# Another order of issue for the first phase of a layernorm, S4D convolution and gMLP kernel

## The chip, the cores and the metric

The kernel runs on one core of a Trainium2 chip. The metric is the device time of one execution in microseconds (us). A core has five engines that issue their own instruction streams in order: TensorE (PE, matmuls, with PEld for its weight loads), VectorE (DVE), ScalarE (ACT), GpSimd (POOL) and SyncE (SP, which here only issues DMA transfers). They wait for one another by semaphores.

## The reference

The input `u` has 2048 positions of 512 channels. A state space model (S4D) gives each channel a kernel K of 2048 taps, and the layernormed input is convolved with it; a gMLP block follows. Cut to what is computed:

```
A = -exp(log_A_real) + 1j * A_imag;  dt = exp(log_dt);  C = (C_real + 1j * C_imag) * dt
K = 2 * real(sum over n of C[d, n] * exp(A[d, n] * dt[d] * l))        # (512, 2048)
h = u + irfft(rfft(ln(u)) * rfft(K)) + ln(u) * D_skip
z = gelu(ln(h) @ w_in);  z1, z2 = halves of z
h2 = h + (z1 * (w_sp @ ln(z2) + b_sp)) @ w_out
```

## The kernel before

The first phase (`phase_a`, to 301.87 us) computes K and the convolution; the later phases, the gMLP, are the same in both kernels. The 512 channels are worked through in four chunks of 128, and a chunk in eight sequences of 16 channels. Fourier transforms are two stages of matmuls with constant matrices. The steps, with the names by which they appear in a row as written tile `<-` read tiles:

- `params` (DVE, ACT, a little POOL) makes the rates and coefficients of the channels' 128 modes, for chunk 0, then chunk 1, then chunks 2 and 3 together; results go through memory and come back by `stack` as `sw`. `table` (POOL, ACT) makes the factors `mt`.
- `norm_x` (DVE statistics, ACT or POOL for most normalising) layernorms u.
- `unit`, 32 of them, eight to a chunk, makes the taps of 16 channels. PE: the phase `ps<-c_k,sw`, two matmuls. ACT rounds, DVE takes the fraction `wb<-wb,ps`, ACT takes sines. POOL multiplies `m` from `mt`. DVE: three multiplies to `f`. PE: the first product `ps<-f`. DVE: the cosine multiply `wa<-ps,wa`, 128x1024. POOL: one more multiply. PE: the second product `ps<-wa,wb`. DVE or ACT: the copy to `ks`. Unit 13 is the sixth unit of chunk 1.
- `piece_a` (first transform stage of the input, PE `ps<-wb,big` for chunks 0 and 1 and `ps<-wb,wa` for 2 and 3, which `xt_load` brings back from memory as `wa<-scr_xhat`) and `piece_b` (second stage, PE `ps<-big,a` or `ps<-trio,a`, `128x64x2`), eight each per chunk, each followed by an evacuation from PSUM.
- `exchange`: eight DMA transfers per chunk on SP, `trio<-trio`, that swap the halves of the partitions. They go out as two groups of four, the second behind the last of the first. The exchange of a chunk needs its `piece_b` and every `piece_e` of the chunk before.
- `piece_c` (first stage of the taps, PE `ps<-wb,ks`, with an evacuation) and `piece_d` (second stage, PE `ps<-big,a`, `128x2x2x32`; then on DVE the spectral multiply `trio<-ps,trio`), which needs all eight `piece_c` and the exchange.
- `piece_e`: the inverse, PE `ps<-c_inv,trio`, 64 matmuls, with an evacuation to `big`. It needs all of the chunk's `piece_d`.

The order of all this is not the order of the code. `Plan` records each operation, 1380 in all, and `schedule` sorts them by a rank from the table `RANKS` (two digits in base 64 for each). `issue` then issues them one by one, so each engine gets its own in that order; every instruction of the phase has the line of `issue`, L249. Operations that two engines can do (evacuations, `ks` copies and the like on ACT or DVE; normalising on ACT or POOL; a few steps of `params` on DVE or POOL) are recorded with `either`, and the table `FORMS` has a digit for each choice. `BANKS` has a digit for each PSUM allocation: 0 and 1 are banks of 2x512 values, 2 to 5 of 512. The schedule touches nothing else; the waits follow from what the operations read and write in that order.

Of the kernel before, what the change touches and what calls it, by code (L numbers as in the profile page):

```python
# [33 lines left out]

DIGITS = "0123456789ABCDEFGHIJKLMNOPQRSTUVWXYZabcdefghijklmnopqrstuvwxyz+-"
RANKS = (
    "0600040901050F080B0A0b0Q0l0I0M070g0W03020C0E0G0H0J0K0L0N0O0R0V0Y0Z0c0U0d0e0n0i0m0q0t0w0z0+1112131416181J1T1w231+2628292D"
    "2E2H2K0y2J0-1K2N2P2b2X2e2V2j2u2z2p1Y1k1o2h2l2-0T0D0P0X0a0S0h0o0k0f331V371C10151W3c3N0s1O1c1r5X0j1p1l0p1j1n1q1g1D1B1U1P1m"
    "1X1b1A0x1H0u1I1h1i0r0v1Z1G1F1a171E1Q1R1u1y222527212A2F2L2O2Q2S2U2W2Y2a2c2d2g2i3I2s3L3Y2m3K3W3M3G2w2+382v423F3Q3l2n4N3V3r"
    "3q4P312r35323R3Z3A3D3T3y3p3O461v1f3B1-1S363E191e3C1x2t241s1z393H1N1d341M1L2q2x302M2G2o2R2I2y2k3J3P3g3k3m3X3s3t3x3z3-4043"  # L40
    "4547494B4D4E4H4G4R4I4T544S4x4h4W4f4M4j4u4m514s4U4V5P4k4o4K4Q5H4r4e4+4X574p4L4c4J4O594Y5a5Z5T6E692C2f2Z3S3e3+414Z4d4g4i4l"
    "4n4t4w5A5C5I5L5U5i5n5l5s5u6P6T4A655O5R6a6l746-777A6t6r6w6+5F5M5d6I797G3b3v4C444F4b6d8u8+909194989A9L9O9d9V9f9o9kAfAhAjAv"
    "AyB1BIAQB59GA5BOBxChCTCOCDC5CbC4CUCMC2CfCWCKCGC8CB9n9i9rAoEBEGBGEIEO555W585J4a4v5N5c5E5K4q4-52564z536U6c727C7n7s6G6N6368"
    "6x767q7-7D7J848h3U3d3i505D5S5Y3f2T205G5B5Q5m5b5g5r608X8i8r3a3h3o5j5q5+5x3j1t2B625y5w6M6J5-6Q6V6k8E8N3n3u4y646B6S6L5o5v6C"
    "6A6F6O6o6X6R6s707L979M3w61666i6v7873676Y6f717B6q7K7H7E7P7T7e9N9S7Q486K8m8w9T6D6W6g6n7F7W7Y6p756y6z7N7R7y7d7g818Q8a8d8o7I"
    "7O7V7b7h7x7v7M7Z7U7o7l7r88827z8B8G8k8x9C7f7k7u838H8L8q7t868A898C8K8-8R8z95999I9U9a7w878F8P8Z8g8l8S8M8I8c8Y8j8p8v8t92969B"
    "9E9J7+7m8b939pA15z6b5h5p5V5f5t6H5e5k6Z6h6j6u6e6m7i7p7S7a8O8V8T8f7c7j7X808J8U858D9m9s9+A79qA2A6AA9g9vACAHA9AD9t9yAbAkAUAc"
    "ALAnAwBNB2BFBTBcBhBsBMBkBpCZ9Z9e9lA4ABAGAK9c9Q9DAVARATAiAaAPAmArAxDBDKAFAJAMASAWAeAZ9Y9K9uAlAXAgBBAqAdBEBLBPCxD1ApAuA-B4"
    "B6BSBCAYAsAzB7B9BDBaBUBJBdBiBrCnD4AtA+B3BVBXBjBgBABZBRBYBeBbCCBnC0CFCNCeE3ECDG9xB0BfB+EMB8BKBQBlBqCPBwBWBmBtB-BvBzC-CdCH"
    "D3D8DCDPDeBHCICRCcCjCvCsC9CQCXCmC+CuD5DACwDHDQDTDaDkCtCzD2D9DJDXDOCoDED6DYDNDFDjDdDbDlDsE5E8EHD7DDDSDZDgDqDmD0DVDMDrDoDi"  # L50
    "DzDtDxE0E4E7EJESDICgDhEAETEk8W8n8e8s9F8y9H9z9P9R9W9X9b9j9hA3AEA89wA09-AIAOANBuCJBoC7CSCYCVCkCLCyC1CAByC3C6CEEcEjEVEbEYEd"
    "EiEpEuEzEoEvEfEnElEtFlFtFdFrF3FDFSFbGTGbFKFYG1GNGHGPGcH9DfDyE2E9EDENEKERDpD-EZEQELEwEUEmEyF9FUGpGwDwE1E6ErExF7F1EXEFEaF8"
    "F2F6FEFBF5FJFLFcGuGzEEEhFIFOFVFmFaEqF0FAFTFXFQFyFuFfF+G2G9GCGUFCFGFNFRFeFqFoFFFPFMFgFhFkFwFzFvG8GDGRGxH3FHEeFWFjGaGyFZFi"
    "FnFxG0G6GBFpG4GAG5GEGIGgGWGLGjGmGtHFHLFsG3G7GFGJGYGQF-GGGSGKGMGkH5GsGXH8HWHbHhHpGOGVGfGoH4HBHGH1GnGvH7H2G+HMHHHPHVHcHjHn"
    "HvGlG-HAHIHNHYHSGdHEHKHOHRHTHdHgHeHmHoHrHtHzGrGhH6I7IDIMCiCrCqCaCpClDLDUDRDWD+DcDnDuDvEPEgEWE+F4EsE-HJHaGZGiIRIcH0HDGeGq"
    "IOIUHQHXHwI3I0I5IFIQILISIIINIBIHI4IAI8IEIGIJIvJ2JuKCJ6JTJYJiJfJoIkJ7IYIgJNJxK2KfHZHfHkHqIKIWIPHUHsHlI2H-HyIfIbIVIiImIxKH"
    "KNHCHiHuH+I6I9IdI1ICHxIjIXInJ0ItIhJ3J9JCKVKgITIZIeIlIpI+IuIaIsIzIqIyJ4JHJDJ1JLJOJRK0K7IrIwI-J5JBJGJQIoJ8JEJAJIJMJmJUJbJp"
    "K4K5KLKxJFJJJPJVJdJnJhJKJSJXJlJaJcK6JtJkKAKYKnKqKwJWJZJeJjJqK1JvJgJ+JwJzK9J-KPKIK8KSKXKcKeKrJrJyK3KBKFKUKRJsKEKJKGKMKQKa"
    "KZKWKiKuKyK+L2KDKKKTKbKhKlKoKOKdKjKkKmKpKvKtKsKzK-L0L1L3L4L6L7LALBLHLGLJLCLFL5L8LELIL9LDLPLSLLLOLXLZLRLULKLMLNLQLTLWLVLY"
)  # L60
# [1214 lines left out]
```

## Time and profile before

| | us |
|---|---|
| median of three runs (839.03 to 842.73) | 839.1 |
| the profiled execution | 842.89 |
| span of its profile | 841.1 |
| first phase, to the first matmul of the next | 301.87 |
| PE, DVE, ACT, POOL busy in the span | 785.9, 650.9, 474.0, 300.7 |
| the same to 302 us | 254.28, 268.52, 246.80, 217.23 |

A row of the table of stretches gives a stretch from A to B in us, its length, the busy time of each engine with its number of instructions, the granted clock of TensorE as a share of full speed, the share of DMA time and GB/s. A row of a group gives the line, engine, operation, written and read tiles with their shape, and the count; behind the first bar the busy time of all in us and the mean of one in ns; behind the second the idle time ahead of them and who ended it. A row of the timeline or of the chain begins with the start and the length in us.

### The profile page before, as it was taken

What the parts mean: (1) busy time and instruction counts of PE and PEld (TensorE: products, weight loads), DVE (VectorE), ACT (ScalarE), POOL (GpSimd) and SP (SyncE); (2) the same over time, 40 slices, a digit from 0 to 9 for tenths busy, and PEclk for the clock granted to TensorE, in tenths of its full rate; (3) what the DMA queues carried; (4) which work ended last, traced back from release to release, by engine and by line L of the source; (5) the groups of instructions that cost most, each with busy time, mean ns of one, the idle gap of its engine ahead of it and who ended that gap; (6) DMA issues with size and microseconds to landing.
All of it is one profiled execution on the core that took longest, in us unless ns stands there. A gap on an engine that the chain in (4) does not pass through costs nothing.

```text
span 841.1 us, 20499 instructions
## 1 busy us (share of the span) xinstructions
PE 785.9 (93%) x8321; PEld 672.9 (80%) x8321; DVE 650.9 (77%) x1234; ACT 474.0 (56%) x795; POOL 300.7 (36%) x352
## 2 busy tenths in 40 slices
PE   0479999899999898999999999999999999999998
PEld 0278889688888898888999988888888878888887
DVE  6999999799998678663377689978856984888533
ACT  5799999789998235355223355555444443454111
POOL 5888959689877000000142100333231002232200
PEclk9999999999999999999999999999999999999999
DMA  9321613402205825445064045899799548799732
GB/s 333 95 104 41 137 40 68 113 19 53 63 3 116 327 54 138 138 138 190 36 151 125 1 150 141 186 222 222 188 209 217 152 140 202 149 249 236 166 111 77
DMA packets 64942, 115.71 MB, mean 138 GB/s; under 512 B 7024, under 2 KB 21488, under 8 KB 63952
## 3 DMA queue, kind: packets, MB, share of 16 engines
q1 hardware_dynamic: 53216, 93.04, 37.0%
q0 software_dynamic: 11632, 21.37, 15.6%
q8 instruction: 65, 1.06, 0.5%
q14 instruction: 29, 0.24, 0.1%
HBM read 86.59 MB, written 19.40 MB: 126 GB/s over the span
## 4 chain that ended last, share of the span: by engine, by line
PE 76%; DVE 11%; DMA 6%; issue 3%; ACT 2%; POOL 1%; SPq 1%; DVEq 0%; ACTq 0%; POOLq 0%
PE m L1163 26%; PE ps L249 24%; PE pz L958 9%; PE pz L852 9%; PE po L1086 5%; DVE trio L249 3%; PE pl L1086 2%; DMA zo<-scr_h 2%; DMA raws<-in_w_sp_dram 2%; DMA wa<-scr_xhat 1%; DMA trio<-in_par_dram 1%; DMA big<-in_u_a_dram 1%; DVE stats L753 1%; DVE big L249 1%; DVE wts L671 1%
## 5 line engine op out<-in xcount | busy, mean ns | idle before, releaser
L1163 PE MATMUL m<-wts,zc_wa 128*128 128x512 f32 x700 | 221.1, 395 | 0.0
L1163 PEld LDWEIGHTS m<-wts,zc_wa 128*128 128x128 f32 x700 | 131.7, 188 | 31.1 <-DVE c L1178 0.2
L1163 PE MATMUL m<-wts,zc_wb 128*128 128x512 f32 x350 | 138.1, 394 | 0.0
L1034 POOL DMA_DIRECT2D raws<-in_w_sp_dram x64 | 58.1, 971 | 212.0 <-DMA raws<-in_w_sp_dram 210.7
L249 POOL TENSOR_TENSOR wa<-mt 128x512 f32<-128x512 f32 x96 | 107.4, 1133 | 18.6 <-PE ps L249 15.4
L670 ACT CAST wts<-raws 128x512 fp32r<-128x512 f32 x112 | 69.0, 619 | 58.9 <-PE m L1163 30.7
L671 DVE TENSOR_TENSOR wts<-raws,wts 128x512 fp32r<-128x512 f32 x112 | 76.4, 684 | 20.0 <-ACT wts L670 19.9
L1163 PEld LDWEIGHTS m<-wts,zc_wb 128*128 128x128 f32 x350 | 65.8, 188 | 15.5
L958 PE MATMUL pz<-w,ht 128*128 128x448 f32 x384 | 77.0, 362 | 0.0
L958 PEld LDWEIGHTS pz<-w,ht 128*128 128x128 f32 x384 | 72.0, 187 | 4.9
L852 PE MATMUL pz<-ht,w1h 128*128 128x512 f32 (+1 forms) x248 | 74.2, 380 | 0.0
L964 POOL TENSOR_SCALAR sm<-sm 128x1 f32<-128x1 f32 x16 | 5.2, 326 | 183.5 <-DVE sm L963 183.5
L249 PEld LDWEIGHTS ps<-c_inv,trio 128*64 128x64 f32 x2048 | 63.0, 141 | 7.8 <-DVE trio L249 4.3
L249 PE MATMUL ps<-c_inv,trio 128*64 128x64 f32 x2048 | 65.4, 226 | 3.5 <-DVE trio L249 3.4
L1086 PE MATMUL po<-w,gz 128*128 128x512 f32 x252 | 61.8, 393 | 1.3 <-DVE zo L1126 1.3
L670 ACT CAST zc_wa<-raws 128x384 fp32r<-128x384 f32 (+1 forms) x70 | 36.9, 532 | 42.5 <-DVE raws L1068 25.6
L249 ACT ACTIVATE wb<-wb 128x1024 f32<-128x1024 f32 (+1 forms) x64 | 56.9, 891 | 0.9
L1086 PEld LDWEIGHTS po<-w,gz 128*128 128x128 f32 x252 | 47.3, 188 | 12.3 <-DVE zo L1126 1.7
L249 ACT ACTIVATE ps<-wb 128x1024 f32<-128x1024 f32 (+1 forms) x64 | 54.6, 859 | 3.1 <-DVE wb L249 1.3
L249 PE MATMUL ps<-big,a 128*128 128x128 f32 x448 | 54.5, 279 | 1.0 <-DVE big L249 0.9
L249 PEld LDWEIGHTS ps<-big,a 128*128 128x128 f32 x448 | 51.4, 192 | 3.5 <-issue 2.0
L852 PEld LDWEIGHTS pz<-ht,w1h 128*128 128x128 f32 x248 | 46.2, 193 | 8.8 <-ACT w1r L801 0.2
(168 smaller groups left out, 1530.0 us busy)
## 6 DMA issues: line engine op xcount, KB each, us to landing
raws<-in_w_sp_dram SPq DMA_DIRECT2D x112, 256.0 KB, 4.0
raws<-in_w_sp_dram POOLq DMA_DIRECT2D x80, 256.0 KB, 6.3
trio<-trio SPq DMA_DIRECT2D x32, 256.0 KB, 4.3
scr_z<-zo SPq DMA_DIRECT2D x28, 256.0 KB, 2.0
big<-in_u_a_dram SPq DMA_DIRECT2D x8, 512.0 KB, 7.3
xq<-in_u_b_dram SPq DMA_DIRECT2D x4, 1024.0 KB, 8.1
scr_h<-xq SPq DMA_DIRECT2D x16, 256.0 KB, 4.6
zo<-scr_z SPq DMA_DIRECT2D x14, 256.0 KB, 4.3
```

Source lines behind the costliest of these rows:

```text
L249: r = getattr(getattr(self.nc, e), method)(*map(self.real, args), **{k: self.real(x) for k, x in kw.items()})
L670: nc.scalar.copy(hi, src)
L671: nc.vector.tensor_sub(lo, src, hi.bitcast(F32))
L753: nc.vector.bn_stats(stats[:, n % 2, i, :], xqs[n % 3][:, i, :])
L852: nc.tensor.matmul(pt[:, w], a[:, q, f], ht[n][k][:, q, w], start=((q, i) == terms[0]), stop=((q, i) == terms[-1]))
L958: nc.tensor.matmul(pt[:, :FQ], a[:, q], w2[:, b, q, f], start=(q == 0 and i == 0), stop=(q == 3 and i == 2))
L964: nc.gpsimd.tensor_scalar_add(sm[:, 14:15], sm[:, 13:14], 1e-5)
L1034: nc.gpsimd.dma_start(r, ws[1], accum_op=ALU.add)
L1086: nc.tensor.matmul(pt, gz[fb][x][:, P * a:P * a + P], wo[:, y, fb, w], start=(first and fb == fbs[0] and i == 0), stop=(last and fb == fbs ...
L1163: nc.tensor.matmul(pt, x[:, f], y, start=(k == 0 and i == 0), stop=(k == KT - 1 and i == 2))
```

## The change

The three tables are replaced; there is no other edit. The operations and what they compute are the same. Each table is one long string, of which one line stands for the rest:

```diff
 RANKS = (
-    "0600040901050F080B0A0b0Q0l0I0M070g0W03020C0E0G0H0J0K0L0N0O0R0V0Y0Z0c0U0d0e0n0i0m0q0t0w0z0+1112131416181J1T1w231+2628292D"
...
+    "08020F0r1I0g0B0G0c0z1B0w1A0h1r3C4V1201000304070D0K0M0O0R0V0W0X0Y0a0d0Z0f0k090s0+0-1C1J1M0A0E0L0N0P0S0T0t0U0u100y1118161L"
...
 FORMS = (
-    "111111110001000111100111101100010000100011101000010011100011010111100000100111111111011010111110000110111101011000011001"
...
+    "111111110100001000101101011001001111110011000101000100100111001011110011011111111111110000011011101110011100010110101011"
...
 BANKS = (
-    "345452345244335544523535253025554240055110423005311052211552013400044010433330224523313242203203321123325421144400252114"
...
+    "335324233355242342422055322542444550040311455014550025210224115240034411252545452334235354545353342223543450123301425013"
```

Counted over the phase, DVE has 454 instructions before and 448 after: 67 evacuations and 54, 12 `ks` copies and 21, two steps of `params` fewer. ACT has 13 evacuations more and nine copies fewer. Around the middle, with the cosine multiply of unit 13 as the dividing point, the orders hold these numbers:

| | before | after |
|---|---|---|
| DVE up to and with that multiply | 303 | 286 |
| of them evacuations, `ks` copies, `params` | 35, 8, 56 | 21, 6, 55 |
| PE from the unit's second product to chunk 2's last `piece_e` | 105 | 130 |
| products, phases | 29, 15 | 33, 16 |
| `piece_a`, `piece_b` | 6, 8 | 11, 16 |
| `piece_c`, `piece_d`, `piece_e` | 13, 16, 16 | 14, 16, 23 |
| small ones | 2 | 1 |

**PE behind chunk 0's `piece_d`.** Before, from its last two `piece_d` on:

```order
L249 MATMUL ps2_100<-big_97,a2_78 128x2x2x32 x4
L249 MATMUL ps3_101<-big_97,a2_78 128x2x2x32 x4
L249 MATMUL ps0_98<-c_k_88,sw0_90 128x512 x2
L249 MATMUL ps2_100<-wb_87,wa_86 64x128 x8
L249 MATMUL ps3_101<-c_inv_60,trio_79 64x64 x32
L249 MATMUL ps2_100<-c_inv_60,trio_79 64x64 x32
L249 MATMUL ps1_99<-c_inv_60,trio_79 64x64 x32
L249 MATMUL ps4_102<-f2_96 32x64 x16
```

After, from some rows behind its last `piece_d` on:

```order
L249 MATMUL ps1_99<-c_k_88,sw1_91 128x512 x2
L249 MATMUL ps4_102<-f0_94 32x64 x16
L249 MATMUL ps3_101<-wb_87,wa_86 64x128 x8
L249 MATMUL ps4_102<-wa_86,wb_87 32x64 x16
L249 MATMUL ps2_100<-f1_95 32x64 x16
L249 MATMUL ps0_98<-c_k_88,sw1_91 128x512 x2
L249 MATMUL ps4_102<-c_inv_60,trio_79 64x64 x32
L249 MATMUL ps2_100<-wa_86,wb_87 32x64 x16
L249 MATMUL ps5_103<-c_inv_60,trio_79 64x64 x32
L249 MATMUL ps4_102<-wb_87,wa_86 64x128 x8
```

Before, the first inverses (`c_inv`) follow two rows behind the last `piece_d`. After, 16 rows stand between, units of chunk 1 and the first stage of chunk 2, and the last `wa,wb` row here is the second product of unit 13: one inverse is ahead of it, where before all eight were.

**DVE ahead of that multiply.** Before, the rows up to the cosine multiply of unit 13 (the last row):

```order
L249 COPY trio_79<-ps5_103 128x64x8
L249 TENSOR_TENSOR f1_95<-ps1_99,wa_86 128x512
L249 COPY big_97<-ps2_100 128x32x16
L249 TENSOR_TENSOR f1_95<-ps1_99,wa_86 128x512
L249 COPY trio_79<-ps3_101 128x64x8
L249 SCALAR_TENSOR_TENSOR f1_95<-wa_86,ps1_99 128x512
L249 SCALAR_TENSOR_TENSOR wb_87<-wb_87,ps0_98 128x1024
L249 COPY ks0_80<-ps3_101 128x256
L249 TENSOR_TENSOR wa_86<-ps5_103,wa_86 128x1024
```

After:

```order
L249 TENSOR_TENSOR wa_86<-ps3_101,wa_86 128x1024
L249 TENSOR_TENSOR f1_95<-ps0_98,wa_86 128x512 x2
L249 SCALAR_TENSOR_TENSOR f1_95<-wa_86,ps0_98 128x512
L249 COPY big_97<-ps5_103 128x128x4
L249 COPY ks0_80<-ps4_102 128x256
L249 SCALAR_TENSOR_TENSOR wb_87<-wb_87,ps1_99 128x1024
L249 TENSOR_TENSOR wa_86<-ps5_103,wa_86 128x1024
```

The evacuations of chunk 2's `piece_b` (`trio_79<-ps`) that stood among the unit's multiplies are no longer here.

**PE at chunk 2's inverses.** Before, the last four of the eight:

```order
L249 MATMUL ps5_103<-c_inv_60,trio_79 64x64 x32
L249 MATMUL ps1_99<-c_k_88,sw1_91 128x512 x2
L249 MATMUL ps4_102<-c_inv_60,trio_79 64x64 x32
L249 MATMUL ps3_101<-c_inv_60,trio_79 64x64 x32
L249 MATMUL ps2_100<-f0_94 32x64 x16
L249 MATMUL ps2_100<-wa_86,wb_87 32x64 x16
L249 MATMUL ps0_98<-c_k_88,sw1_91 128x512 x2
L249 MATMUL ps3_101<-c_inv_60,trio_79 64x64 x32
```

After:

```order
L249 MATMUL ps0_98<-c_k_88,sw1_91 128x512 x2
L249 MATMUL ps1_99<-c_k_88,sw1_91 128x512 x2
L249 MATMUL ps5_103<-c_inv_60,trio_79 64x64 x32
L249 MATMUL ps2_100<-c_inv_60,trio_79 64x64 x32
L249 MATMUL ps3_101<-c_inv_60,trio_79 64x64 x32
L249 MATMUL ps4_102<-c_inv_60,trio_79 64x64 x32
L249 MATMUL ps0_98<-f0_94 32x64 x16
L249 MATMUL ps3_101<-f1_95 32x64 x16
```

All phases of chunk 3 now stand ahead of the last four inverses, and the exchange of chunk 3 follows on them as before.

More of the change, by code (lines that the diff above doesn't have):

```diff
@@ L36 @@
 RANKS = (
-    "0600040901050F080B0A0b0Q0l0I0M070g0W03020C0E0G0H0J0K0L0N0O0R0V0Y0Z0c0U0d0e0n0i0m0q0t0w0z0+1112131416181J1T1w231+2628292D"
-    "2E2H2K0y2J0-1K2N2P2b2X2e2V2j2u2z2p1Y1k1o2h2l2-0T0D0P0X0a0S0h0o0k0f331V371C10151W3c3N0s1O1c1r5X0j1p1l0p1j1n1q1g1D1B1U1P1m"
-    "1X1b1A0x1H0u1I1h1i0r0v1Z1G1F1a171E1Q1R1u1y222527212A2F2L2O2Q2S2U2W2Y2a2c2d2g2i3I2s3L3Y2m3K3W3M3G2w2+382v423F3Q3l2n4N3V3r"
-    "3q4P312r35323R3Z3A3D3T3y3p3O461v1f3B1-1S363E191e3C1x2t241s1z393H1N1d341M1L2q2x302M2G2o2R2I2y2k3J3P3g3k3m3X3s3t3x3z3-4043"
@@ L41 @@
[L41 to L56, printed above, removed]
@@ L57 @@
-    "KNHCHiHuH+I6I9IdI1ICHxIjIXInJ0ItIhJ3J9JCKVKgITIZIeIlIpI+IuIaIsIzIqIyJ4JHJDJ1JLJOJRK0K7IrIwI-J5JBJGJQIoJ8JEJAJIJMJmJUJbJp"
-    "K4K5KLKxJFJJJPJVJdJnJhJKJSJXJlJaJcK6JtJkKAKYKnKqKwJWJZJeJjJqK1JvJgJ+JwJzK9J-KPKIK8KSKXKcKeKrJrJyK3KBKFKUKRJsKEKJKGKMKQKa"
-    "KZKWKiKuKyK+L2KDKKKTKbKhKlKoKOKdKjKkKmKpKvKtKsKzK-L0L1L3L4L6L7LALBLHLGLJLCLFL5L8LELIL9LDLPLSLLLOLXLZLRLULKLMLNLQLTLWLVLY"
+    "08020F0r1I0g0B0G0c0z1B0w1A0h1r3C4V1201000304070D0K0M0O0R0V0W0X0Y0a0d0Z0f0k090s0+0-1C1J1M0A0E0L0N0P0S0T0t0U0u100y1118161L"
@@ new lines @@
+    "1O1T1U131c1X1n1j1m1p1o261x2X2i2h2a0n0v14191D1i05060J0C0I0H0j0Q0i4A0l4E2x211W1K292O4b2E2M1q2N5p241s1+1z1l1w1N1f0m0e201P22"
+    "0o0p0b1t151F1Q0x1-0q1G251k1H1E231S1d1R2H2J2K2L2T2S2d2e2f2k2n2p2r2u3235383D3F3I3a3g41523x3y4N3V3i4M3S4x3m3w564k4h4j4d3c4L"
+    "3R4K4O3k706U476z3j3K3J3M3P3h7d3G2c2w2I2V2Q2o2F2P3W2Y332y2v343N3T3A2C2W2+2l1V3X2Z2R2U3E3Z2B2q2G3d3e3f3o3p4g3+3-404246494B"
+    "4D4F4J4T4Y4f4n4u4y4z586m7f5m7S6g536I7g7J7Q5I5B716A4q4w5Z4p5t4o5z4r7O6s5W6l7c7I6f7T5b5H8U7n898V9s171Z1u1v2j2t3L3O1Y1b1a1e"
@@ new lines @@
+    "1g1h1y27282A2D2s3U3n4C4I4U4a4v4i6H3z4G5J6Q6e6k746v7v6S739I4X2b5R5U6W6Y4P5d4-505+686M6p6r5g605l676E6X6o6x6w6y7H7C7U7k7e7l"
+    "7z84857sAXAHAwAxBkCFBmCdCjBzBlCXC8EnExFMF5CiFIEuDU8w9V9f9h9yA19gEcEd595F5w65646F5S5h5s5v5A5X5Q5Y5n5q6i6j6J6R6K6L7L7m6a6b"
+    "6t6u8B8M6-7R8a8u3136373Q3Y4W3r2z3H393u3l3v4c4l3s4m4s5T878L2-303b3q3t4t4Q2m3B2g4Z48434+5C4R5L5N7B8R8T44454S4e5E5G5i4H5554"
+    "5O5K5V5x5o5u616N6O979851575D5P5e6B6D5M5c5f5a5j5r6T6C6G6V6h7p8b8i78828e8g8p8q5k5y666d6n7D6+5-636276756q7P7E7M7Z7t7u8G8N69"
@@ new lines @@
+    "6P6Z727N7W7+6c797A777G7F8A7X7-8C8S8h9C9D7K7V7b7y8I8O8K7Y7j7o868F8D8r8P8j8s8t909O9c7a7w808E8J8+8d8H8m8Y8v8n8o9F8-969G9H9Y"
+    "9j9kAB9zAQAVAhAt8k8l7q7r81838W8X7h7i7x888Z8z9E9KA+B69q9rB9BA9iA0AMAWA2ADA4ARAEAOATAnASAZA3A5B0B1AmAv9t9u9w9xAGAKCaClDhDi"
+    "DDDECGCHDRDeDXDYC6C7D8D9EjEp8Q8c8f939J9M9P8y94999A959B9b9N9e9o9pArBLBM8x91929T9d9lA99L9W9Z9U9X9aAc9mAAAdA-BSBhBi9Q9R9SA7"
+    "ACAbAFAI9vA6ALAJA8AgAkAYAlApBjDlDm9n9+9-ANAPB7AaAeAiAjAoAyAzBQB8AqBRBXBpCmD2CzCcAfCbCtCuAUB2B3BEBWBYBcAuAsB5BGBHBOBrBaBu"
@@ new lines @@
+    "BvBwDJEDEUBBBCBDBbB-C0C1B4BZBTBeBgBfB+C2CACBCTDuECESBqBsBxCCCOCVCeByC9CICDCECJCnCWCfCvCyDvEEEJC3C4C5CMCgCpCqCKCRCPCNCUCQ"
+    "CoCsCrD3DHDPE4E5EBDFEGEREmFLBFBJBIBKBPBNBUBVBdBnBoCYBtCLCSCZCkE1ChCwDOE6E7F3EWEXFGFHFQFdFPFTF6F7FBFCEPEZFUFaF9FAEeEqFRFf"
+    "EbErGCGDFEFFFWF-GAGBGkGvHXHkGbGrHTHZHSHVHcHsHaHbGTGUIbIiC-D4D5DGDSDVDgD0D1CxDNDKDIDpDWDqDwDxFZGGGHC+DADBDLDTDjDZD6DCD7DM"
+    "DQDfDrDkDaE2E3FrGSGnDbDcDdDsDtD-EfDzEAE0D+EHEFEhEIEgEsEzG5GNGODnDyE8E9EVElEaDoEKENEMELETEiEoEkEvE-F4I7IBH3GeEQGKGtGwEOEY"
@@ new lines @@
+    "E+F8FJFgFKFYFXEtFmFeFNFzFvFnG0G2HyICIDF0F1F2FDFVFlFjFOEyEwFqFpFSF+FyFxG3G4GfI3I4FsFwG8G9GJGPGYG6G1GMGQGLGhGqGpGuGzH0HFIN"
+    "IOFtG7GIGWGXGoGdGaGRGVGlGjGiGmGsGgGxGyHEIFIGFuHDI6HYIqJNFhFoFiFbFkFcGEGFGZGcH2HIHGHHHtHJHLHKIQIVIRIaIcIgJJJKJ5JEJOJPJ4J6"
+    "JHJIJQJRJVJWJ2J3IjIrJLJMIYIwIfImJBJDIhJ7IZIlKJKjK7KLJeJyJYJrK9KUJfK5JZJgK8KVKSKTH6H7HMHNHeHmHgH1G-H8HPHQHOHqHnHhHvI1KiKm"
+    "KnH5H9HAHBHdHoHiG+H4HCHRHUHWHuHpHjHzI8I9KcKuHlHrH-I0IAIJIUI2HwH+IIIHIPIpISItIuIvKwKyKzHfHxI5IEIdIeInIMITIKIXIWILIsIkIoIx"
@@ L60 @@
+    "J0J1KrKsIzJ9JTJUJXJiJbJkJFJCJnJmJlJoJuJpJvJxK-L0L1I+I-JAJGJSJtJaJcJ8IyJdJjJhJsJwJzJ-KHKOKdKeK1K2K3KDKKKkKfJqKNK0KQKPKEKR"
+    "KlKgKoKpKqKtKvK6KAKBKFKGKMKaJ+KCK4KIKXKWKZKYKbKhKxK+L2L3LHLJLFLGL4L5LDLELALIL9LCL8LBL6L7LOLPLMLNLLLULSLTLYLZLKLXLVLWLQLR"
 )
 FORMS = (
-    "111111110001000111100111101100010000100011101000010011100011010111100000100111111111011010111110000110111101011000011001"
-    "001011010110000001001101101011101101001001000011111111010111010100110111010000100100001100101001011101100100010000000110"
@@ L64 @@
-    "010111"
+    "111111110100001000101101011001001111110011000101000100100111001011110011011111111111110000011011101110011100010110101011"
+    "111010010000001011011100011101100011100010001010010010100010111010100010110011000110000100001100000000111011101111001011"
+    "010101"
 )
 BANKS = (
-    "345452345244335544523535253025554240055110423005311052211552013400044010433330224523313242203203321123325421144400252114"
-    "340055200435115230025311352524324022325345045255203254433350043210523113220045411434005231033511242203423245225454431323"
@@ L69 @@
-    "5253334323511554004401154400223104201155200455114243534225443422535"
+    "335324233355242342422055322542444550040311455014550025210224115240034411252545452334235354545353342223543450123301425013"
+    "530022411343005221133400123454234542234235242534542022535431154300524105521114500554112320055311412325324422245332351430"
+    "5244524335211345002320055311544005141104500405115322453524325425345"
 )
```

## The prediction

> **What bounds the kernel now.** I read the table of stretches first, because the change touches nothing after 301.87 us, where the first matmul of the next phase starts.
>
> ```profile
> core 0: us, PE busy (x) PEld busy (x) DVE busy (x) ACT busy (x) POOL busy (x), PEclk, DMA share, GB/s
> 67.00:96.00 29.00, 29.00 (x585) 26.32 (x580) 28.90 (x43) 28.89 (x44) 26.99 (x29) 1.00 0.40 84
> 101.00:154.00 53.00, 52.44 (x1188) 46.96 (x1184) 50.65 (x69) 49.73 (x63) 40.05 (x42) 1.00 0.31 70
> 173.00:260.00 87.00, 86.45 (x2204) 77.62 (x2208) 84.05 (x103) 80.99 (x100) 72.42 (x75) 1.00 0.15 34
> 0.00:154.00 154.00, 116.08 (x2278) 102.49 (x2278) 142.04 (x305) 134.95 (x212) 121.98 (x141) 1.00 0.41 119
> 259.00:302.00 43.00, 37.34 (x964) 34.72 (x960) 29.04 (x33) 17.00 (x28) 10.24 (x13) 0.96 0.66 217
> ```
>
> The reader is to see a first phase in which nothing has slack. From 67 to 96 us PE is busy for all of 29.00 us and DVE for 28.90; from 173 to 260 PE for 99% and DVE for 97%; ACT follows within 7%. Three engines near full at once is possible only if the order gives each of them its share of work at every moment. So an order is judged by whether one engine's work is bunched early and another's late: then each in turn becomes the bound while the other waits.
>
> The chain of waits shows the same from the other side:
>
> ```profile
> 116.73 37.80 PE ps L249 x1041
> 154.53 3.29 DMA wa<-scr_xhat
> ...
> 183.89 50.13 PE ps L249 x1222
> ...
> 236.09 23.71 PE ps L249 x792
> ...
> 277.42 6.88 DVE trio L249 x6
> 284.35 16.86 PE ps L249 x512
> ```
>
> From 116 us on the chain runs on PE, with a wait of 3.29 us for a transposed input. Its last two links are the close of the phase: the multiplies of the last chunk's piece_d, then its eight piece_e.
>
> **The mark.** To compare the orders I take one instruction that both have in the middle, the cosine multiply of unit 13 on DVE, the 14th of its kind on DVE in both. Behind it comes the second product of the unit on PE:
>
> ```profile
> 152.30 0.41 DVE L249 COPY ks<-ps 128x256 f32<-128x256 f32 x1
> 152.63 1.21 DVE L249 TENSOR_TENSOR wa<-ps,wa 128x1024 f32<-128x1024 f32 x1
> 153.76 0.68 DVE L249 TENSOR_TENSOR f<-ps,wa 128x512 f32<-128x512 f32 x1
> 154.03 0.65 PE L249 MATMUL ps<-wa,wb 128*32 128x64 f32 x32
> 256.81 2.08 PE L249 MATMUL ps<-c_inv,trio 128*64 128x64 f32 x64
> ```
>
> The multiply ends at 152.63 + 1.21 = 153.84, the product starts 0.19 later, and chunk 2's last piece_e ends at 256.81 + 2.08 = 258.89. The phase cannot be shorter than DVE's work up to the mark plus PE's work from that product on, since each engine issues in order and the product needs the multiply. The counts on both sides are in the table with the change.
>
> **DVE up to the mark.** It issues 303 instructions before and 286 after: 14 evacuations fewer (35, 21), two ks copies fewer (8, 6), one of params fewer; the rest is equal.
>
> ```profile
> L249 DVE COPY big<-ps 128x512 f32<-128x512 f32 x43 | 29.2, 684 | 10.2 <-PE ps L249 10.1
> L249 DVE COPY trio<-ps 128x512 f32<-128x512 f32 (+1 forms) x26 | 16.3, 644 | 0.6 <-PE ps L249 0.6
> L249 DVE COPY ks<-ps 128x256 f32<-128x256 f32 x12 | 5.0, 416 | 0.4 <-PE ps L249 0.3
> L249 DVE TENSOR_SCALAR trio<-trio 128x128 f32<-128x128 f32 (+3 forms) x9 | 3.1, 344 | 0.1
> ```
>
> 14 by 0.67 is 9.4, two by 0.416 is 0.8, one by 0.34: 10.5 us. Neighbours overlap a little (152.63 is 0.08 before 152.30 + 0.41), so I take 10.0. The stretch to 154 us holds 142.04 of DVE work, so DVE is idle for 12.0. With the same idle the mark comes at 143.8. If half the idle goes, as it may where the first unit's inputs are computed earlier, it comes at 137.8; if all but 4 us of it goes, at 135.8. If the start gains 3 us of waits (the first parameters now stand ahead of the normalisation, and their steps alternate between DVE and ACT), at 146.8. I take 143.8.
>
> **PE from the mark to chunk 2's last piece_e.** 105 blocks before, 130 after. What went to DVE's early half came out of PE's: before the mark PE now does one piece_e of chunk 0 instead of eight, and chunk 2's piece_b all come after it. Each block is priced by its weight loads, the phase by its matmuls:
>
> ```profile
> L249 PEld LDWEIGHTS ps<-c_inv,trio 128*64 128x64 f32 x2048 | 63.0, 141 | 7.8 <-DVE trio L249 4.3 <-issue 1.8 <-ACT wb L249 0.7
> L249 PEld LDWEIGHTS ps<-big,a 128*128 128x128 f32 x448 | 51.4, 192 | 3.5 <-issue 2.0 <-ACT big L249 0.4 <-DVE trio L249 0.2
> L249 PEld LDWEIGHTS ps<-trio,a 128*128 128x128 f32 x64 | 7.7, 191 | 0.9 <-DVE ks L249 0.4 <-DVE trio L249 0.2
> L249 PEld LDWEIGHTS ps<-wb,ks 128*64 128x64 f32 x512 | 28.7, 138 | 3.9 <-issue 1.4 <-POOL ks L249 0.8 <-DVE ks L249 0.4
> L249 PEld LDWEIGHTS ps<-wb,big 128*64 128x64 f32 x256 | 16.2, 152 | 7.2 <-DVE big L249 6.0 <-ACT trio L249 0.5 <-issue 0.4
> L249 PEld LDWEIGHTS ps<-wb,wa 128*64 128x64 f32 x256 | 14.7, 141 | 5.8 <-DMA wa<-scr_xhat 3.3 <-DVE trio L249 0.9 <-issue 0.8
> L249 PEld LDWEIGHTS ps<-f 128*32 128x32 f32 x1024 | 15.7, 109 | 6.3 <-issue 2.7 <-ACT wb L249 0.7 <-ACT ps L249 0.5
> L249 PEld LDWEIGHTS ps<-wa,wb 128*32 128x32 f32 x1024 | 16.4, 110 | 3.2 <-POOL wb L249 2.5 <-issue 0.5
> L249 PE MATMUL ps<-c_k,sw 96*128 96x512 f32 x64 | 24.6, 474 | 2.5 <-DVE wb L249 2.4 <-DMA sw<-scr_stk 0.2
> L249 PEld LDWEIGHTS ps<-c_k,sw 96*128 96x128 f32 x64 | 10.6, 205 | 6.0 <-DVE wb L249 3.3 <-issue 0.8 <-DVE big L249 0.2
> L249 PEld LDWEIGHTS ps<-trio,c_mean 128*128 128x128 f32 x16 | 3.9, 325 | 17.2 <-DVE trio L249 17.0
> ```
>
> One piece_e is 63.0/32 = 1.97 us; piece_b and piece_d (51.4 + 7.7)/64 = 0.92; piece_c 28.7/32 = 0.90; piece_a (16.2 + 14.7)/32 = 0.97; a product (15.7 + 16.4)/64 = 0.50; a phase 24.6/32 = 0.77; a small one 3.9/16, some 0.3 with its partners. The difference: 7 piece_e are 13.8, 8 piece_b 7.4, 5 piece_a 4.9, 4 products 2.0, one phase 0.8, one piece_c 0.9, one small one less 0.3: **+29.4 us**. In all it was 97.8 and is 127.2.
>
> How well do such sums tell time? For the blocks that start from 67 to 96 us they give 28.98 where the stretch is 29.00, from 101 to 154 us 52.54 for 53. Before's 97.8 took 258.89 - 154.03 = 104.9; without the 3.29 for the transposed input 101.6, a ratio of 1.04, with DVE a second bound beside PE. After, DVE has slack in that half, so I take the ratio of 101 to 154 us, 1.01: 128.5. Ends: weights alone for the phases, (24.6 - 10.6)/64 = 0.22 less for each of 32 matmuls, 127.2 - 7.0 = 120.2; and 1.04, 132.3.
>
> **The close.** Chunk 3's exchange cannot start before chunk 2's last piece_e is evacuated, in both orders: the last of the eight is sequence 1 before and 0 after, and both lie in the part that the first transfer overwrites.
>
> ```profile
> 258.98 10.22 SPq L249 DMA_DIRECT2D trio<-trio  x8
> 275.15 9.14 DVE L249 TENSOR_TENSOR trio<-ps,trio 128x1024 f32<-128x1024 f32 x8 [1.31 <-PE ps L249]
> 284.35 16.84 PE L249 MATMUL ps<-c_inv,trio 128*64 128x64 f32 x512 [2.98 <-DVE trio L249]
> ```
>
> From 258.89 the exchange takes to 275.15 before the first multiply may run, eight multiplies take 9.14, eight piece_e 16.84. What else stands there now is four products and eight piece_c, 4 x 0.50 + 8 x 0.90 = 9.2 us of PE: hidden in 16.3. So these 43 us move as a whole; I cost them at nothing, at most 2 either way for the loads of the next phase that share the queue.
>
> **The edits that cost nothing by themselves.** 13 evacuations go from DVE to ACT and nine ks copies from ACT to DVE over the phase, which is 13 x 0.67 - 9 x 0.416 = 5.0 off DVE, and two params steps go to POOL, 0.7. ACT has 259 - 154 - 94.85 = 10 us free behind the mark. If that cover is gone it is at most 13 x 0.58 - 9 x 0.37 = 4.2 us, by these rows:
>
> ```profile
> L249 ACT COPY big<-ps 128x512 f32<-128x512 f32 x45 | 25.9, 582 | 32.0 <-PE ps L249 31.6
> L249 ACT COPY ks<-ps 128x256 f32<-128x256 f32 x20 | 7.3, 373 | 1.3 <-PE ps L249 1.3
> ```
>
> The new banks add no instruction. A bank that is taken before its reader is done makes a PE wait; before, the chain shows none of over 1 us from 183.89 to 234, and I keep this in the upper end.
>
> **The sum.** 143.8 + 0.2 + 128.5 = 272.5 against 258.9: +13.6 us. The profiled run was 842.89 (span 841.1) and would be 856.5; the median of the runs is 839.1, 3.8 below it, so 852.7, say **852.5**. Lowest: 135.8 + 0.2 + 120.2 = 256.2, -2.7, all gains at once. Highest: 146.8 + 0.2 + 132.3 = 279.3, +20.4, 859.5.
>
> **A rule to weigh.** The Trainium skill, page "Perfetto Trace Analysis", section "Optimization Strategy", says that where the most contended engine changes between regimes of a kernel, interleaving those regimes may improve it. The trace agrees: PE and DVE at 99% and 97% in one stretch is such an interleaving, and by that rule the new order, which parts them, loses. The same page, "Identifying the Most-Contended Engine", calls matmul busy time a poor measure and wants weight-load time for PE but occupancy for DVE. By that rule DVE at 97% and not PE at 89% bounds 173 to 260 us, and the second case below is what it gives, 833.
>
> **The rivals.**
> *Slower, by PE's late work* (the forecast), 843.5 to 860: 0.62.
> *Faster: DVE stays the bound all through.* The extra 25 PE blocks fit in PE's gaps and only DVE's 5.7 us less count: 839.1 - 5.7 = 833. For it: weight loads fill only 77.62 of 87 us. Against it: PE would have to do the 127.2 in 258.9 - 5.7 - 144.0 = 109.2 us, 0.86 of the sum; the weight loads alone of those blocks are 120.2. It decides when a block costs under 0.86 of its row, or when the mark comes before 126. 0.09.
> *No change, about 839:* the mark at 136 and PE at 122, so 136 + 0.2 + 122 = 258.2. For it: 12 us of DVE idle before the mark. Against it: most of that lies in the first loads. 0.12.
> *Slower still: the exchanges show.* Chunk 1's and 2's exchange take some 16 us each, as above (258.89 to 275.15). The PE work that the new order has between a chunk's last piece_e and the next multiply is about 14 us behind chunk 0 and 12 behind chunk 1, so 2 + 4 us of wait on top, and what DVE lacks meanwhile: 8 in all, 860.6, up to 866. It decides when that work is under 16 us. 0.17.
>
> The lowest 2 in 10 or so are cut at 838 (the faster case is left out), the top at 864. A measurement of this kernel can tell some 0.5% from no change: faster is below 834.9, slower above 843.3. From the cases: faster 0.09, within 0.13, slower 0.78.
>
> **What would show it.** In the profile after: the 14th cosine multiply on DVE ending near 144 us, not near 154; chunk 2's last piece_e ending near 272; the stretch between with PE over 97% and DVE below 92%; the close 43 us as before. Wrong would be a mark at 136 or earlier, or PE blocks at under 0.95 of their sum; a hole on PE that ends in a DVE multiply ahead of chunk 1's or 2's piece_e would be the fourth case.

## The result, and the profile after

| | before | after |
|---|---|---|
| median, us | 839.07 | 859.72 |
| ratio, with its 95% interval | | 1.0235 (1.0207 to 1.0263) |
| span of the profile, us | 841.1 | 858.9 |
| first phase, to the first matmul of the next, us | 301.87 | 318.44 |

The new order is slower by 20.6 us, 2.35%, where 13.4 were forecast. How it comes about is not how the prediction had it. The profiled executions took 842.89 and 860.62 us, 3.8 and 0.9 above their medians, so the spans differ by 17.8 us and not by 20.6.

The table of stretches after, with the columns of before:

```profile
67.00:96.00 29.00, 24.74 (x501) 21.02 (x502) 29.00 (x46) 28.08 (x45) 27.03 (x34) 1.00 0.49 134
101.00:154.00 53.00, 50.22 (x1192) 44.96 (x1190) 49.80 (x64) 51.48 (x67) 50.27 (x51) 1.00 0.20 51
173.00:260.00 87.00, 85.85 (x2193) 81.50 (x2193) 74.63 (x92) 75.12 (x94) 64.04 (x66) 1.00 0.19 46
260.00:284.00 24.00, 17.58 (x400) 15.91 (x396) 8.54 (x13) 9.22 (x16) 3.56 (x8) 0.99 0.82 250
284.00:302.00 18.00, 8.42 (x70) 8.23 (x71) 9.33 (x8) 0.94 (x1) 0.00 (x0) 0.59 0.55 180
0.00:138.80 138.80, 92.39 (x1671) 77.45 (x1671) 127.69 (x288) 121.80 (x198) 118.72 (x141) 1.00 0.38 112
138.80:265.40 126.60, 124.38 (x3295) 117.00 (x3293) 110.25 (x143) 113.19 (x143) 96.96 (x99) 1.00 0.24 57
```

The reader is to see the balance gone: from 67 to 96 us DVE is busy throughout and PE for 24.74 of 29.00 us, later PE is at 98% and DVE at 87%. And something new: from 284 to 302 us nearly nothing runs, and PE's granted clock is 0.59.

The mark, on the timelines of DVE and PE after, with the last two inverses of chunk 2, the first multiplies of the last chunk and the close:

```profile
137.30 1.22 DVE L249 TENSOR_TENSOR wa<-ps,wa 128x1024 f32<-128x1024 f32 x1
...
138.82 0.65 PE L249 MATMUL ps<-wa,wb 128*32 128x64 f32 x32
...
259.81 3.55 PE L249 MATMUL ps<-c_inv,trio 128*64 128x64 f32 x112
...
289.91 4.62 DVE L249 TENSOR_TENSOR trio<-ps,trio 128x1024 f32<-128x1024 f32 x4 [15.63 <-DMA trio<-trio]
291.19 6.68 PE L249 MATMUL ps<-big,a 128*128 128x128 f32 x32 [12.32 <-DVE trio L249]
300.26 16.70 PE L249 MATMUL ps<-c_inv,trio 128*64 128x64 f32 x512 [2.39 <-DVE trio L249]
318.44 1.82 PE L734 MATMUL y<-big,g 128*64 128x128 f32 x29 [1.49 <-ACT big L249]
```

So the profiled time parts like this:

| stretch | before, us | after, us | difference |
|---|---|---|---|
| to the product behind the mark | 154.03 | 138.82 | -15.2 |
| from there to chunk 2's last inverse | 258.89 - 154.03 = 104.9 | 263.36 - 138.82 = 124.5 | +19.7 |
| close, to the next phase | 301.87 - 258.89 = 43.0 | 318.44 - 263.36 = 55.1 | +12.1 |
| later phases | 841.1 - 301.87 = 539.2 | 858.9 - 318.44 = 540.5 | +1.2 |

The sum is 17.8, the difference of the spans. The first two, which the prediction was about, leave 4.5; the close, which it costed at nothing, brings 12.1. The chain of waits shows where:

```profile
265.24 5.82 DMA trio<-trio
272.87 16.75 DMA trio<-trio
291.19 5.50 PE ps L249 x24
296.72 3.50 DVE trio L249 x3
300.26 14.86 PE ps L249 x448
```

And SP's timeline, where the DMA transfers are issued:

```profile
212.97 53.49 SPq L249 DMA_DIRECT2D trio<-trio  x12
266.55 1.15 SPq L695 DMA_DIRECT2D xq<-in_u_b_dram  x1
267.81 1.19 SPq L698 DMA_DIRECT2D g<-in_c_g_dram  x1
269.10 0.40 SPq L695 DMA_DIRECT2D xq<-in_u_b_dram  x1
269.55 0.55 SPq L698 DMA_DIRECT2D g<-in_c_g_dram  x1
271.07 2.39 SPq L249 DMA_DIRECT2D trio<-trio  x4
273.56 11.71 SPq L705 DMA_DIRECT2D w1r<-in_w_dram  x4
```

Before, all eight transfers of the last exchange went out ahead of the next phase's loads. Now the second four go out behind two `xq` and two `g`, 4 MB, and the last of them takes 16.75 us. The loads are issued outside the recorded plan, and in the program as built they stand ahead of four transfers that still wait for the first half.

### The profile page after: what moved, and what is told of

Read it like the earlier page. It is cut to its first block, busy times and chain, and to the rows that moved or that the text cites. A ratio compares the mean times of both kernels' runs of the same rounds, so it can differ in the third digit from the quotient of the medians.

```text
span 858.9 us, 20510 instructions
## 1 busy us (share of the span) xinstructions
PE 784.5 (91%) x8321; PEld 674.4 (79%) x8321; DVE 641.5 (75%) x1228; ACT 471.8 (55%) x794; POOL 302.2 (35%) x357
## 4 chain that ended last, share of the span: by engine, by line
PE 69%; DVE 12%; DMA 7%; ACT 5%; POOL 3%; issue 2%; SPq 1%; DVEq 0%; ACTq 0%
PE m L1163 29%; PE ps L249 14%; PE pz L958 9%; PE pz L852 9%; PE po L1086 6%; DVE trio L249 3%; DMA trio<-trio 3%; PE pl L1086 2%; ACT wb L249 2%; DVE f L249 1%; ACT ps L249 1%; POOL wa L249 1%; DVE big L249 1%; DVE wb L249 1%; ACT big L249 1%
## 5 line engine op out<-in xcount | busy, mean ns | idle before, releaser
L1163 PE MATMUL m<-wts,zc_wb 128*128 128x512 f32 x350 | 138.0, 394 | 0.0
L249 POOL TENSOR_TENSOR wa<-mt 128x512 f32<-128x512 f32 x96 | 106.5, 1130 | 10.5 <-PE ps L249 8.5
L1163 PEld LDWEIGHTS m<-wts,zc_wb 128*128 128x128 f32 x350 | 65.8, 188 | 15.4
L249 PE MATMUL ps<-big,a 128*128 128x128 f32 x448 | 55.9, 286 | 13.6 <-DVE trio L249 12.3
L249 PEld LDWEIGHTS ps<-big,a 128*128 128x128 f32 x448 | 54.2, 201 | 15.1 <-DVE trio L249 12.5
L249 PE MATMUL ps<-c_inv,trio 128*64 128x64 f32 x2048 | 63.7, 225 | 2.4 <-DVE trio L249 2.4
L249 PEld LDWEIGHTS ps<-c_inv,trio 128*64 128x64 f32 x2048 | 62.6, 141 | 4.0 <-DVE trio L249 2.6
L249 ACT ACTIVATE ps<-wb 128x1024 f32<-128x1024 f32 (+1 forms) x64 | 54.7, 864 | 4.3 <-DVE wb L249 3.8
L249 ACT ACTIVATE wb<-wb 128x1024 f32<-128x1024 f32 (+1 forms) x64 | 55.3, 889 | 0.2
```

Source lines behind the costliest of these rows:

```text
L249: r = getattr(getattr(self.nc, e), method)(*map(self.real, args), **{k: self.real(x) for k, x in kw.items()})
L1163: nc.tensor.matmul(pt, x[:, f], y, start=(k == 0 and i == 0), stop=(k == KT - 1 and i == 2))
```

## The experiments

Where the text says "with the loads behind", the base is the first experiment's kernel, so that the close is out of the way. Each kernel was timed beside the kernel before on its chip, and a ratio is to that.

**The queue.** The changed kernel, where the loads may not be placed ahead of the second half:

```diff
+    def behind(r):
+        info = mybir.DependencyInfo(mybir.DependencyClass.NoSync, mybir.DependencyReason.SCHED_ONLY)
+        tc.add_manual_dep(r.ins, rest(None), info, reason="behind the exchange")
...
-        nc.sync.dma_start(xqs[n % 3], uv[:, 16 * n:16 * n + 16])
+        behind(nc.sync.dma_start(xqs[n % 3], uv[:, 16 * n:16 * n + 16]))
```

(the same for `g` and `w1r`; `rest(None)` names the second half.)

> The changed kernel, with one edit: the loads of the next phase are ordered behind the second half of the last exchange on SP's queue, without a wait. Queue theory (4 MB of loads that now stand ahead of that half make it land 18.5 us after issue in place of 8.2, and this is most of the longer close, 55.1 us against 43.0): the close comes back to 43 to 45 us, the time falls by 10 to 12 us to 848 to 850 us. Rival (the close is longer because PE runs at a lower granted clock there, 0.59 from 284 to 302 us, and has more work left): falls by less than 3 us, 857 to 860 us.

Measured 848.28 us, ratio 1.0090 (1.0058 to 1.0122), 11.4 us below the changed kernel. SP's timeline and then DVE's:

```profile
264.49 10.20 SPq L249 DMA_DIRECT2D trio<-trio  x8
274.78 1.14 SPq L702 DMA_DIRECT2D xq<-in_u_b_dram  x1
...
278.84 9.14 DVE L249 TENSOR_TENSOR trio<-ps,trio 128x1024 f32<-128x1024 f32 x8 [3.67 <-DMA trio<-trio]
```

The first multiply starts at 278.84 where it was 289.91, and the close is 307.3 - 264.4 = 42.9 us, as before the change. The queue theory holds, and the rival falls. The reverse is the kernel before with the second half behind those loads. Here `rest(None)` issues it, and the order of SP's loads is fixed as it is written:

```diff
         for o in order[:cut]:
-            nc.issue(o)
+            if o is not second:
+                nc.issue(o)
...
+        if between is None:
+            return nc.issue(second)
...
+    with tc.manual_schedule(engines={mybir.EngineType.SP}):
+        load_x(0)
+        load_g(0, 16)
+        load_x(1)
+        load_g(16, 48)
+        rest(None)
```

> The kernel before, with the second half of the last exchange behind the first four loads of the next phase on SP's queue. Queue theory: its close grows from 43 to some 54 us and the time by 10 to 12 us, to 849 to 851 us, with nothing else of the change in it. Rival (the order of the loads does not matter, the rest of the new order does): within 3 us of 839 us.

Measured 853.96 us, ratio 1.0173 (1.0127 to 1.0218): 14 us, more than expected. Its SP and DVE say why:

```profile
257.66 3.02 SPq L249 DMA_DIRECT2D trio<-trio  x4
260.79 1.14 SPq L699 DMA_DIRECT2D xq<-in_u_b_dram  x1
269.94 0.36 SPq L702 DMA_DIRECT2D g<-in_c_g_dram  x1
270.39 1.70 SPq L699 DMA_DIRECT2D xq<-in_u_b_dram  x1
272.14 0.42 SPq L702 DMA_DIRECT2D g<-in_c_g_dram  x1
272.66 3.53 SPq L249 DMA_DIRECT2D trio<-trio  x4
...
294.00 4.62 DVE L249 TENSOR_TENSOR trio<-ps,trio 128x1024 f32<-128x1024 f32 x4 [21.00 <-DMA trio<-trio]
```

Here the first `g` stood on the queue until 269.94, when PE had done a first product (`ps<-f`) that it waited for, so the second half went out 15.0 us behind the first (272.66 - 257.66), where it was 7.6 in the changed kernel. The close was 62.0 us (319.60 - 257.58) in this profile, of an execution of 859.41 us, 5.5 above the median. So four loads on a queue, with the wait of one of them, cost this much with nothing else of the change; what the wait alone costs was not measured.

**The two halves together.** Both kernels, with the halves of the last exchange no longer one after the other:

```diff
-        nc.ops[-1]["after"] = nc.ops[-2]
+        if c + 1 < NCH:
+            nc.ops[-1]["after"] = nc.ops[-2]
```

> The kernel before, where the second half of the last exchange no longer waits for the first. If the halves wait for one another for nothing (a half is 1 MB and takes 7.2 us, with DMA engines free), both land after 9 to 11 us in place of 15.4 and the close falls by 4 to 6 us: 833 to 835 us. If the transfers fill the DMA engines, both land after 15 us and the time stays at 839 us.

> The changed kernel, where the second half of the last exchange no longer waits for the first; by this its four transfers also come ahead of the next phase's loads on SP's queue. Queue theory with free DMA engines: 12 + 4 to 6 us less, 842 to 844 us. Queue theory with full DMA engines: 10 to 12 us less, 848 to 850 us. Rival that the close is longer for PE's sake: 857 to 860 us.

The kernel before: 838.5 us, ratio 0.9984 (0.9965 to 1.0003), which does not show a gain. The changed kernel: 846.38 us, 1.0082 (1.0053 to 1.0111), the gain of the queue and hardly more. By its semaphore in the trace the last transfer landed 13.3 us behind the first issue in the kernel before (269.05 - 255.72), where it was 15.4 (274.41 - 258.98), and 12.7 in the changed one (276.46 - 263.78), where it was 14.0 with the loads behind (278.52 - 264.49). That is 2.1 and 1.3 us earlier, where free DMA engines were to give 4 to 6. In the kernel before, not even these 2 us can show, because the exchange does not end the last wait. PE's piece_d and DVE's first multiplies there, with both halves on the way:

```profile
271.08 7.38 PE L249 MATMUL ps<-big,a 128*128 128x128 f32 x64 [0.88 <-DVE big L249]
272.25 9.14 DVE L249 TENSOR_TENSOR trio<-ps,trio 128x1024 f32<-128x1024 f32 x8 [1.31 <-PE ps L249]
```

The exchange has landed 3.2 us earlier; the multiply waits for PE, and PE for the evacuation of piece_c by DVE. So the expected 4 to 6 us are not there, in this kernel for that reason too.

**Is PE the bound behind the mark?** Half of the sum of 16 piece_e is left out, in both orders:

```diff
+        n = 1 if c in (1, 2) else 2
...
-                    for i, t in enumerate(spectra(c)[:2]):
+                    for i, t in enumerate(spectra(c)[:n]):
```

> The changed kernel with the loads behind the exchange, where each piece_e of chunks 1 and 2 leaves out the half of its sum from its second spectrum: 32 matmuls in place of 64, some 0.98 us less of PE for each, 15.7 us in all, all of it behind the mark. Prediction's theory (PE is the bound from the mark to chunk 2's last piece_e, 99% busy there, while DVE has 110 of 127 us): the time falls until DVE binds, by 9 to 14 us, 834 to 839 us. Rival (the chain there runs through DVE, ACT and the exchanges, and PE is busy only because it is always fed): less than 4 us, 844 to 849 us.

> The kernel before with the same left out. The same 15.7 us less of PE; DVE is at 97% there, so by the prediction's theory only what DVE has free counts, 3 to 7 us: 833 to 837 us, clearly less than the changed kernel gains. If PE alone is the bound in this order too, 9 to 14 us, as in the other.

Measured 842.95 us, ratio 1.0055 (1.0038 to 1.0073), from 1.0090; and 835.59 us, ratio 0.9964 (0.9945 to 0.9983). So 15.7 us of PE bring 3 to 5 us in one order and 3 in the other, and the new order does not gain clearly more. The result is weakened by a wait that the edit also removes: the exchange of the next chunk need no longer wait for those inverses (chunk 3's went out at 246.3, where it was 264.5). A cleaner one takes PE work away and no wait:

```diff
-            for j in range(4):
+            for j in range(2 if c >= 2 else 4):
                 nc.tensor.matmul(pt[:, :, 2 * j:2 * j + 2], a2v[:, 4 * g + j, :],
```

> The changed kernel with the loads behind the exchange, where the 16 piece_b of chunks 2 and 3 leave out two of their four products: 16 x 0.46 = 7.4 us less of PE, all of it behind the mark, with the same waits. PE theory: 5 to 7.4 us less, 841 to 843.5 us. Exchange theory: only what lies between a multiply and the inverses counts, 0 to 3 us less.

Measured 845.23 us, ratio 1.0083 (1.0054 to 1.0112): 0.6 us by the ratios, 3 by the medians, of 7.4. The intervals leave room for some 4 us, not for the 5 to 7.4 of the PE theory. That PE is 98% busy there does not make it the bound for most of the stretch.

**Is DVE the bound up to the mark?** The same multiply left out of eight units, early or late (18 to 25); what stands in `left` is not issued. In the third kernel POOL's last multiply to `m` is left out in the same way:

```diff
-        nc.vector.tensor_mul(f3[:, 2, :], sn, m[:, 1, :])
+        o = nc.vector.tensor_mul(f3[:, 2, :], sn, m[:, 1, :])
+        if 6 <= su < 14:
+            left.append(o)
```

> The changed kernel with the loads behind the exchange, without the third f multiply of units 6 to 13: 8 x 0.68 = 5.4 us less of DVE, all of it ahead of the mark. Prediction's theory (DVE is the bound up to the mark, and PE's work behind it then starts earlier as a whole): 4 to 5.5 us less, 843 to 844.5 us. Rival (DVE's early work is not what the end waits for): less than 1.5 us.

> The changed kernel with the loads behind the exchange, without the third f multiply of units 18 to 25: the same 5.4 us less of DVE, all of it behind the mark. Prediction's theory (DVE has slack there): within 1.5 us of 848.3 us. Rival (DVE binds all through): 4 to 5.5 us less.

> The changed kernel with the loads behind the exchange, without the last of the three POOL multiplies to m in units 6 to 13: 8 x 1.13 = 9.0 us less of POOL, all of it ahead of the mark. Taking 5.4 us of DVE away there moved the mark by 0.7 us only. If POOL binds there (28.8 of 29 us busy from 96 to 125), the mark comes 4 us or more earlier, and the time falls with it by 3 us or more. If ACT binds (28.4 and 28.1 of 29 us), or the three are tied, less than 2 us.

The ratios are 1.0104 (1.0073 to 1.0136), 1.0105 (1.0071 to 1.0139) and 1.0115 (1.0076 to 1.0154): none is faster than the base's 1.0090. Intervals this wide exclude a gain of 4 us, but not one of 2. The late edit came out as the prediction's theory has it (DVE has slack there). The mark stood at 138.7 and stands at 138.0 without the DVE work and at 139.0 without the POOL work; in the kernels whose early half is not edited at all it lies between 137.3 and 139.2. In the profile without the DVE work the granted clock was 0.88 from 67 to 96 us, so that the mark alone would prove little; the times of its other three executions, 844.5 to 848.6 us, are those of the base, 845.2 to 849.2. DVE, busy for 29.00 of 29.00 us from 67 to 96, is not what the mark waits for by itself, and neither is POOL.

**Do the exchanges lie on the chain?** Chunk 0's inverses end at 159.8 and chunk 1's first multiply starts at 175.1, so it looked like it. The exchanges of chunks 1 and 2 are not issued:

```diff
         nc.ops[-1]["after"] = nc.ops[-2]
+        if c in (1, 2):
+            left.extend(nc.ops[-2:])
```

> The changed kernel with the loads behind the exchange, without the exchanges of chunks 1 and 2 (16 transfers left out). Exchange theory (chunk 0's inverses end at 159.8 us in place of 137.9, so that the exchanges of chunks 1 and 2, 14.4 us each from the last inverse to the first multiply, now lie on the chain): the time falls by 6 us or more, 842 us or less. PE theory of the prediction (PE is fed with other work meanwhile and binds): less than 2 us, 846 to 848.5 us.

> The kernel before without the same exchanges. Exchange theory: chunk 1's multiplies start 19 us after its exchange has landed, chunk 2's 8 us, so nothing waits: within 1.5 us of 838.5 to 840 us. If the exchanges cost something in this order too, 3 us or more.

Measured 845.52 us, ratio 1.0079 (1.0050 to 1.0109), from 1.0090; and 836.62 us, 0.9968 (0.9953 to 0.9984). The exchange theory falls: chunk 1's first multiply moves from 175.1 to 173.4 only, about as far as it lies from the 174.0 of the changed kernel itself. The kernel before gains as much, some 3 us, more than expected there.

**What stays put in all of these** is chunk 2's first multiply. DVE's timeline, with the loads behind (the last figure counts only multiplies that begin within the window shown):

```profile
232.19 2.35 DVE L249 TENSOR_TENSOR trio<-ps,trio 128x1024 f32<-128x1024 f32 x2
```

Without the early DVE work:

```profile
232.05 2.34 DVE L249 TENSOR_TENSOR trio<-ps,trio 128x1024 f32<-128x1024 f32 x2
```

Without the early POOL work:

```profile
232.14 2.35 DVE L249 TENSOR_TENSOR trio<-ps,trio 128x1024 f32<-128x1024 f32 x2
```

Without the two exchanges:

```profile
230.64 3.47 DVE L249 TENSOR_TENSOR trio<-ps,trio 128x1024 f32<-128x1024 f32 x3
```

Before the change it starts earlier:

```profile
226.89 3.49 DVE L249 TENSOR_TENSOR trio<-ps,trio 128x1024 f32<-128x1024 f32 x3
```

Without the PE work it comes at 231.77 (less of piece_b) and 230.75 (half of the inverses of chunks 1 and 2), and in the changed kernel itself, with nothing left out, at 231.04. From this multiply to chunk 2's last inverse it takes 258.89 - 226.89 = 32.0 us before and 264.4 - 232.2 = 32.2 with the loads behind, and the close is 43 in both. So the 5.3 us by which this multiply is late are the whole difference of those two spans (846.4 - 841.1). The size of the lag depends on the profile: before's has TensorE at a granted clock of 0.58 from 159 to 163 us, and in the two other kernels that do all the same up to there (the last halves together, the loads ahead) the multiply starts at 222.8 and 225.6. So the lag is 5 to 9 us, and the medians of the two kernels differ by 8.4 (848.28, 839.91). The multiply needs every unit of chunk 2.

The chain of waits shows where the units are held in the early half. From 67 to 139 us, before and then in the changed kernel (the view ends the row there):

```profile
by line: PE ps L249 89.2%; DMA wa<-scr_xhat 7.3%; DVE trio L249 3.3%; issue 0.4%; DVEq L249 0.0%
```

```profile
by line: PE ps L249 17.9%; POOL wa L249 13.2%; ACT wb L249 12.9%; DMA wa<-scr_xhat 9.6%; ACT ps L249 8.9%; POOL mt L249 6.9%; POOL wb L249 6.9%; ACT big L249 6.5%; issue 5.1%; ACT mt L249 2.8%; POOL big L249 2.8%; ACT L249 1.8%; ACT trio L2
```

Where the chain ran on PE (for 66% in the kernel before with the last halves together), it now runs on ACT from 67 to 94 us, but for some 3 us, then mostly on POOL to 119.7, and hardly on DVE. A chain names one path: with 9.0 us less of POOL the mark stayed, so another path of about the same length must lie beside it. The one engine whose work none of the experiments lessened is ACT. Its rows, before and then with the loads behind:

```profile
67.00:227.00 160.00, 155.70 (x3560) 139.22 (x3556) 150.68 (x205) 147.83 (x194) 132.15 (x139) 0.99 0.30 69
```

```profile
67.00:227.00 160.00, 149.22 (x3601) 135.16 (x3602) 146.60 (x199) 151.27 (x202) 143.90 (x153) 1.00 0.33 82
```

ACT was third of the five columns and is now the fullest. By the time that it has evacuated the last of chunk 2's piece_c (225.56 and 228.88 us), ACT has been busy for 197.8 us before and for 205.6 with the loads behind: 14 more of its operations are of units, 17 of chunk 3's where it was 3, and seven more are evacuations, against two loads of function tables (`ACT_TABLE_LOAD`, 1.28 us each), three `ks` copies and three other steps fewer. That is 7.8 us of ACT work more ahead of a multiply that comes 5 to 9 later. POOL has 14.9 us more by then (181.2, 196.1), but in the stretch above it is still the least busy of the four. That ACT sets the pace is an argument from counts, from the chain, and from what was left when the others fell; no kernel with less work on ACT was run. The rival is that no engine does, and that the units go round through four nearly full engines, each of which delays the next. Between the two it is open.

## Why the prediction was right or wrong, point by point

- **Slower, and by about how much:** right in sign; 852.5 forecast, 859.72 measured. That the number is near is luck in good part: the two stretches that it was about came out 9.1 us shorter than forecast, and 12.1 of the 17.8 us come from a place that it costed at nothing.
- **The close.** This is the step that failed: "So these 43 us move as a whole; I cost them at nothing, at most 2 either way for the loads of the next phase that share the queue." They grew to 55.1. The step thought of the loads as sharing the queue, and did not look at which of them the new order lets in ahead of the exchange's second half. The order of SP's rows, which is known without a run, has the four loads between `trio` x12 and `trio` x4. Two experiments, one each way, show the mechanism. The step also took the exchange for what the first multiply waits for; in the kernel before, its own row names PE, [1.31 <-PE ps L249], 0.7 us behind the landing.
- **The mark.** Forecast 143.8, came at 138.5. The counts held: the durations of DVE's instructions up to it sum to 148.8 us where it was 159.9, 11.1 less. But the time that they cover fell by 14.5, from 141.9 to 127.4: neighbours overlap by 21.4 us in all and not by 18.0. The step had let the overlap shrink, by 0.5.
- **DVE binds up to the mark:** refuted in the changed kernel; 5.4 us less of DVE moved it by 0.7 and the time not at all.
- **PE from the mark to chunk 2's last inverse.** 130 blocks by the same rows were 127.2 us and took 124.5, a ratio of 0.98 where 1.01 was taken. The sum of rows is good. That PE alone binds there is not: 0.6 to 3 of 7.4 us came back. The 32 us from chunk 2's first multiply on are the same in both orders, and they are not PE's alone either: with 7.8 us less of inverses they were still 29.5 (260.25 - 230.75).
- **Sum of the two:** forecast +13.6 for both, measured +4.5, the mark 5.3 and PE's stretch 4.0 too long.
- **The rivals.** The faster one decides "when a block costs under 0.86 of its row": it was 0.98, so it fell. The no-change one needed a mark at 136 and PE at 122 us: the kernel with the loads behind came to 138.7 and 125.5 and is 0.9% slower, so with the close as before the time lies between this case and the forecast. The one with exposed exchanges fell for chunks 1 and 2, where leaving them out brings 1 to 3 us in either order; an exposed exchange did decide, but chunk 3's, by the queue.
- **Signs named beforehand.** The mark near 144, chunk 2's last inverse near 272 and a close of 43 us did not come true (138.5, 263.4, 55.1). PE over 97% and DVE below 92% behind the mark did (98% and 87%), and proved less than was claimed. The Trainium skill, page "Perfetto Trace Analysis", section "Identifying the Most-Contended Engine", says that matmul busy time does not tell how near PE is to its limit; the runs agree, with 98% busy and 7.4 us less work worth 0.6 to 3 us. For VectorE the Trainium skill goes by occupancy there, and calls the engine with the highest the one to optimise first. Here a measurement differs: DVE was busy for 29.00 of 29.00 us, more than any other engine, and 5.4 us less of its work there and shortly after did not shorten the time.

No version here that does all of the work is shown to be better than the kernel before: the one with both halves together is at 0.9984 with 1 inside its interval. The two below 1 (0.9964 and 0.9968) leave work out. The best use of the new order, with the queue mended, is 0.8 to 0.9% behind.

## What to carry to other kernels

When an order changes, compare the transfer queue's rows to the end of the phase and past it: work of the next phase that is placed by itself may slip ahead of a transfer that waits, and 4 MB there cost 11 to 14 us. Where four engines are each some 90% busy or more, a busy share does not name the bound: take a little work off each in turn, and look for the instant that does not move. Look also at where another profile of the same order has that instant; here it differed by some 4 us. A sum of rows over blocks gave a stretch of 125 us to 2%, but whether it is on the path only a run could tell.

## What the runs showed that was not expected

A 256 KB transfer of the exchange took 16.75 us behind 4 MB of loads, where such a transfer has a median of 4.3. And in the gap that followed, PE's granted clock fell to 0.59 from 284 to 302 us; the eight piece_e behind it took 16.70 us all the same, 16.84 before. The granted clock was 0.90 during them in both; in the kernel before with both halves together it was 1.00, and they took 15.15.
